# A fused attention and state-space kernel on one core: the causal masks of two head groups of segment 2 move to TensorE, and the written order changes in many small places

## The chip, the cores and the metric

The kernel runs on one core of one Trainium2 chip. The core has TensorE (matmuls, here PE, its weight loads PEld), VectorE (DVE), ScalarE (ACT), GpSimd (POOL) and SyncE (SP), which here only issues DMAs. Each engine works through its own list of instructions in order and waits on semaphores for the others. The metric is device microseconds of one execution of the whole program; lower is better.

## The reference, cut to what matters

Two branches read the same input x (2048 tokens, 512 channels), and a gate per token mixes them.

```python
def reference(...):
    g = sigmoid((x * gate_w).sum(-1, keepdims=True))
    a = _A_ref(x, wq, wk, wv, wo, beta)      # attention with a memory, 32 heads of 16
    b = _B_ref(x, ...)                       # state-space kernel K, long convolution, + u * Dskip
    return g * a + (1 - g) * b

# in _A_ref, for each of 4 segments s of 512 tokens:
    logits = einsum('bhqd,bhkd->bhqk', qs, ks) * scale + mask   # mask: -1e9 where query < key
    p = softmax(logits); a_dot = einsum('bhqk,bhkd->bhqd', p, vs)
    a_mem = (phi(qs) @ M) / (phi(qs) @ z + 1e-6)
    o = sigmoid(beta) * a_mem + (1 - sigmoid(beta)) * a_dot
    M, z = M + phi(ks)^T vs, z + sum(phi(ks))
# in _B_ref:
    K = (C * exp(dt*A*l) * dB summed over 128 states).real      # 512 channels x 2048 taps
    y = irfft(rfft(pad(u)) * rfft(pad(K)))[:2048]
```

## The kernel before, in words

**Two streams in one program.** The attention works by segment s (0 to 3) and group of eight heads hg (0 to 3). For each: projections of k and q (project, L1051), tokens' v (seg_tokens, L985), state update (seg_state, L1009), scores, exp, value matmuls and normalisation (scores, L1080), memory part and transposition of the output (ophase, L1270). The state-space branch computes powers of the poles (ssm_powers, L840), tables for the kernel K from them (tables, L1316, four chunks c, with "lag" matmuls), and a long convolution in three levels: a first level over all of x, stored to a scratch in HBM (x_level1, L908), then 32 blocks u (conv, L1406 on), each with a forward transform X, a kernel transform K (E for the first halves), a product Y on VectorE, an inverse V, and a store of V into one of two collecting tiles. The function finals forms sixteen output blocks: fin (first part of the attention output and skip), fir (collected inverses of blocks 0 to 15), fih (last group of heads), fis (those of blocks 16 to 31, so that it needs the last V), out (scaling). For the first eight of the sixteen blocks a half result is spilled to a tile by VectorE (xD, spl) so that the bank comes free; the other eight hold their bank.

**Scores.** A block of scores is written by TensorE into banks 0 to 3 (always these four), exp on ScalarE moves it to a tile pT in SBUF, and the value matmuls read pT. The other four banks serve all else. In segments 0 and 1 (4s + hg < ND) a variant called halves skips the masked half of the diagonal squares. In segments 2 and 3 five blocks per group of heads are worked, in an order that the list fixes: A0 and A1 (one diagonal square of 128 columns per row group), B0, C and B1 (two squares). The causal mask of a block is put on either before the exp by TensorE (the identity times the tile negm, which holds -30000 where the key is later) or after it by VectorE (pT times mask01):

```python
    pem = 4 * s + hg < NPM                                                       # L1089
            op("PE", c_pe("R", ...), f, r=[qT, kT, ko], w=[P], acq=[pT])         # L1228
            if pem:
                    for r in range(4):                                           # L1231
                        st = ent[1][2] if len(ent) > 1 else 0
                        i = mm(e, ap(P, r * 512, [[st, len(ent)], [1, 128]]), ap(ident, n=128),
                               ap(negm, dims=[[0, len(ent)], [1, 128]]), False, True)
            o = op("ACT", ("Ax", 2048), lambda e, ...: e.activation(pT, P, ACT.Exp, scale=0.25), r=[P], w=[pT])   # L1237
            if not pem:
              op("DVE", ("V2", 128 * nb), lambda e, ...: e.tensor_tensor(pT, pT, mask01, ALU.mult), r=[mask01], w=[pT])  # L1248
```

Matmuls of all kinds go through one helper (mm, L706), evictions from PSUM through another (evac, L225 on: L229 is ScalarE's copy, L230 VectorE's, L232 and L233 the scaled ones), and DMAs through a third (L225). So those lines gather many uses.

**The order.** build_graph makes 1808 operations and numbers them as it makes them. What each engine does in which order is written out in the string ORDER (from L375): one entry per operation, in one line of time for all engines. An entry is the number, then a or v where the operation may run on ScalarE or VectorE, then the buffers that it takes. `30/2` is operation 30 with buffer 2, `31a` operation 31 on ScalarE. Sched.replay (L238) walks the list: every engine's list, SP's DMA queue among them, is the entries of that engine in this order. Sched.emit (L267) turns the dependences, and the reuse of buffers and banks, into semaphore waits. A DMA that has to wait in SP's list holds all DMAs behind it.

Numbers that the prediction speaks of: 76, 88, 108 are shifts of the first, second and fourth pole power between partitions (SBUF to SBUF DMAs, pwc0.0, 0.1, 0.3; 108's power has index 3); 626 and 841 are the transposing loads of x for segments 2 and 3; 23 is the load of wk; 6 a small constant (ones); 1246 the store of the first-level result xl1.1, 1253 the eviction of xl1.3; 654 to 657 are scores, exp, mask and values of block A0 of segment 2, group 0, and so on up to 729 for group 1's B1; 1689 to 1692 are Y30, V30, V30's eviction and store.

Of the kernel before, what the change touches and what calls it, by code (L numbers as in the profile page):

```python
# [369 lines left out]
NPM = 8  # L370
# [11 lines left out]
141/6 214a 120 21 139/1 223a 228/0/0/0 1252/2/0 201 229 627/5 628 208/0 1253a 1257/0 140 1040v/0 1039v 1250a 216/3  # L382
217a 224 268 1044 225 1037v 1251 1038v 230 842/1 843 130v/6 271/2/1/1 413/1 256/0/0 1042/0 257 1045 151/2 152/7 1254/3
131 1041 153 132 258 231 311/0/2/2 143 1043 89/3 272 233/0/1 234 165/2 227 188 235 1255a 226 154v/7 269/1/1 238/0/2
239 1049 166v/8 312a 144 202/0 1050 270a 155 90 8/0 1237/3/1 156 1046 273 236/0 240 1239/1 1240a 237 241 99/1 1238a
1256 167 242/0/3 168 203/0 243 244 274 1051 1263/2/0 1264a 1047/0 1052 1265/1 101/3 1266a 163/2 357/3/2 287/0/1 288
1053 245 209/0 1048 100 246 1241 416/2 1278/1 289 417a 247/1 1056/0 358a 232/1/0 275 1054 276/0 250/0/3 251 252 400/2
401 1268/3/1 248 164 1270/1 249/0 175a/9 314/2/0 315a 253/0 254 1269a 283/0/3 284 1061 255 259 1055 1271a 1267 4/0 285
1260/2/0 1261a 1272 1258/3 176 177 1057 1259a 278/0/2 279 280 1062 1262 260 261/2 1273/1/1 1275/2 1276a 313 354/3/3/1
355a 316/2/0/0 1274a 1277 1063 301/0/0 1058 262 302 317 1059/0 281/3 263 264 303 403/0 1286/1/0 1287a 282 286 290 402  # L390
291 359/0/1/1 1060 360 319 318 1065 1066/0 295/0/2 292/3 1294/2/1 1295a 296 297 28/0 1067 320/1 361 1296/2 362 363
1068 1069/0 338/0/1 339 1299/0 293 1064 191/0 109/0 1070 1297a 364 1298 192/0 340 1071/2/0 1075/1 1076 1077 204 111/4
110 121/3 294/1 1079/0 1080 1081a 123/0 1072 1078a 205 1073 1074a 1083/0 1086v/0 1088a 1284/3 1285a 1090v/0 122 298/0
356 1087v 299 300 1094 1092/0 1089v 1095 136a/4 330/0/2 331 332 1085 135/6 112v/2 1091 304 1288 133/1 1279/1/1 472/2/1
473a 113 114 1093 305 321/0/3 1099 306/4 1084 1096 322 323 134 145/2 1100 1097/0 1082 405/3/1/0 406a 341/2 342 307
344/0/0 345 1281/3 346 1101 1280a 476/0 308 309 1098 1282a 1283 1102 420/0 1106/0 421a 326/0/1 327 426/1/0/0 146/7 328
# [138 lines left out]
def build_graph(nc, es, A_x, A_wq, A_wk, A_wv, A_wo, A_beta, B_A_re, B_A_im, B_B_re, B_B_im,  # L535
# [544 lines left out]
    def scores(s, hg, k0):  # L1080
# [7 lines left out]
        nv = {0: 0, 1: 0}  # L1088
        pem = 4 * s + hg < NPM  # L1089

# [558 lines left out]
```

## Time and profile before

| what | value |
|---|---|
| time, median of 3 runs | 292.19 us (289.7, 292.19, 292.36) |
| span of the profiled execution, first to last instruction | 287.5 us |
| that execution's own time | not recorded beside the span; the three runs are 2.2 to 4.9 us above it |
| mean granted TensorE clock | 0.987 |
| ScalarE exps of 2048 columns (L1237, segments 2 and 3) | 40, 76.0 us, 1899 ns each |
| VectorE mask multiplies (L1249, segments 2 and 3) | 40, 22.6 us, 577 ns each |
| evictions by ScalarE (L229) and VectorE (L230), all shapes | 155 and 49 |

Reading it: a row of a group has line, engine, operation, output and input with shape, count, then busy time, the mean length of one in ns, and the idle time ahead of them with what ended it. Matmuls are pipelined, so one's length contains latency that the next one covers. The chain is the work that ended last, followed backwards. In a table of stages each engine has its busy time and, in brackets, its count of instructions.

### The profile page before, as it was taken

The page shows a single profiled execution, that of the slowest core. Times are in us where ns is not written, and L with a number is a line of the kernel's source. Part 1 is how long each engine was busy: PE and PEld are TensorE (multiplying, and loading weights), DVE is VectorE, ACT ScalarE, POOL GpSimd, SP SyncE. Part 2 cuts the span into 40 slices and gives each one's busy share as a digit, 9 for nine tenths or more (in the row PEclk, how much of TensorE's full clock was granted, in tenths as well). Part 3 has the DMA queues.
Part 4 walks back from the last instruction along what each step waited for, and adds up shares of the span by engine and source line. Part 5 has one row for each costly group of instructions (what it writes and reads, how often), then busy time and mean ns, then how long its engine had stood idle before and what let it go on. Part 6 is the DMA issues. An engine that isn't in the chain of part 4 may idle for free.

```text
span 287.5 us, 9336 instructions
## 1 busy us (share of the span) xinstructions
PE 253.1 (88%) x3896; PEld 158.7 (55%) x3947; DVE 265.0 (92%) x617; ACT 254.6 (89%) x320; POOL 5.0 (2%) x10
## 2 busy tenths in 40 slices
PE   5767888787898989979999989999999999999992
PEld 2424454564556546756766657665555454555661
DVE  3998999999999999979999999999999999997782
ACT  5998999999999999989989999999999999983212
POOL 5000000000000000000000000000000000000000
PEclk9999899999999999979999999999999999999999
DMA  6996762421125256914643388585776795894224
GB/s 164 270 223 143 184 203 84 130 87 42 41 47 134 63 141 205 226 32 97 188 132 102 90 252 244 166 232 161 234 215 168 207 229 160 243 186 102 72 109 182
DMA packets 60187, 44.49 MB, mean 155 GB/s; under 512 B 36209, under 2 KB 53490, under 8 KB 60146
## 3 DMA queue, kind: packets, MB, share of 16 engines
q1 hardware_dynamic: 60146, 43.90, 57.0%
q8 instruction: 31, 0.51, 0.8%
q14 instruction: 10, 0.08, 0.1%
HBM read 22.09 MB, written 7.86 MB: 104 GB/s over the span
## 4 chain that ended last, share of the span: by engine, by line
ACT 35%; PE 28%; DVE 26%; issue 5%; DMA 3%; SPq 0%; DVEq 0%; ACTq 0%
PE psum L706 28%; ACT sb L1237 10%; ACT sb L229 10%; ACT sb L1190 8%; DVE sb L1346 7%; DVE sb L1355 3%; ACT sb L850 3%; DVE sb L230 2%; DMA sb<-sb 2%; DVE sb L1349 2%; DVE sb L1487 2%; DVE sb L1358 2%; DVE sb L1249 1%; DVE sb L1154 1%; ACT sb L1021 1%
## 5 line engine op out<-in xcount | busy, mean ns | idle before, releaser
L706 PE MATMUL psum<-sb 128*128 128x17 bf16 (+17 forms) x3808 | 247.4, 229 | 23.5 <-ACT sb L1190 7.4
L706 PEld LDWEIGHTS psum<-sb 128*128 128x128 bf16 (+6 forms) x3859 | 153.5, 102 | 115.5 <-issue 20.7
L229 ACT ACTIVATE sb<-psum 128x512 bf16<-128x512 f32 (+4 forms) x155 | 87.7, 624 | 7.6 <-PE psum L706 6.4
L1237 ACT ACTIVATE sb<-psum 128x2048 bf16<-128x2048 f32 x40 | 76.0, 1899 | 2.1 <-PE psum L706 1.7
L1190 ACT ACTIVATE sb<-psum 128x2048 bf16<-128x2048 f32 (+1 forms) x40 | 70.1, 1751 | 2.8 <-PE psum L706 2.7
L1346 DVE TENSOR_TENSOR sb<-sb 128x4096 bf16<-128x4096 bf16 (+3 forms) x24 | 37.7, 1569 | 0.0
L230 DVE CAST sb<-psum 128x512 bf16<-128x512 f32 (+1 forms) x49 | 29.9, 626 | 1.1 <-PE psum L706 0.9
L1355 DVE TENSOR_TENSOR sb<-sb 128x512 bf16<-128x512 bf16 (+1 forms) x48 | 25.0, 537 | 0.1
L1249 DVE TENSOR_TENSOR sb<-sb 128x1024 bf16<-128x1024 bf16 (+1 forms) x40 | 22.6, 577 | 0.2
L1487 DVE TENSOR_TENSOR sb<-sb 128x1024 bf16<-128x1024 bf16 x32 | 21.6, 685 | 0.9 <-ACT sb L229 0.5
L1349 DVE TENSOR_TENSOR sb<-sb 128x2048 bf16<-128x2048 bf16 (+3 forms) x24 | 20.7, 861 | 0.0
L232 ACT ACTIVATE sb<-psum,sb 128x512 bf16<-128x512 f32 x6 | 4.0, 687 | 12.3 <-PE psum L706 12.3
L1154 DVE TENSOR_TENSOR sb<-psum,sb 128x256 bf16<-128x256 f32 x32 | 13.3, 417 | 0.3
L1358 DVE TENSOR_TENSOR sb<-sb 128x512 bf16<-128x512 bf16 (+1 forms) x24 | 12.9, 536 | 0.0
L850 ACT ACTIVATE sb<-sb 128x512 f32<-128x512 f32 x18 | 11.8, 660 | 0.0
L1151 DVE RECIPROCAL sb<-psum 128x16 f32<-128x16 f32 x32 | 7.9, 252 | 1.8 <-PE psum L706 1.7
L1291 DVE TENSOR_TENSOR sb<-psum,sb 128x512 bf16<-128x512 f32 x12 | 8.2, 687 | 0.2
L858 ACT ACTIVATE sb<-sb 128x512 bf16<-128x512 f32 x12 | 8.0, 683 | 0.0
L1072 ACT ACTIVATE sb<-sb 128x512 bf16<-128x512 bf16 x12 | 8.0, 663 | 0.0
L1021 ACT ACTIVATE sb<-psum 128x512 bf16<-128x512 bf16 x12 | 7.8, 646 | 0.0
L852 DVE SCALAR_TENSOR_TENSOR sb<-sb 128x256 f32<-128x256 f32 x18 | 7.5, 424 | 0.0
L851 DVE TENSOR_TENSOR sb<-sb 128x256 f32<-128x256 f32 x18 | 7.5, 423 | 0.0
(78 smaller groups left out, 122.3 us busy)
## 6 DMA issues: line engine op xcount, KB each, us to landing
sb<-sb SPq DMA_DIRECT2D x64, 128.0 KB, 3.2
sb<-c_DN SPq DMA_DIRECT2D x32, 224.0 KB, 3.0
scr_Z<-sb SPq DMA_DIRECT2D x16, 256.0 KB, 3.2
sb<-scr_Z SPq DMA_DIRECT2D x16, 256.0 KB, 3.6
sb<-in_A_x_dram SPq DMA_DIRECT2D x5, 512.0 KB, 4.6
sb<-c_DN SPq DMA_DIRECT2D x16, 160.0 KB, 3.3
out_dram<-sb SPq DMA_DIRECT2D x8, 256.0 KB, 2.1
scr_O<-sb SPq DMA_DIRECT2D x12, 128.0 KB, 2.7
```

Source lines behind the costliest of these rows:

```text
L229: fa = lambda e: e.activation(dst(), src(), ACT.Copy)
L230: fd = lambda e: e.tensor_copy(dst(), src())
L706: mm = lambda e, o_, l, r_, st, sp, **kw: e.matmul(o_, lhsT=l, rhs=r_, start=st, stop=sp, skip_group_check=True, **kw)
L850: op("ACT", ("As", 512), lambda e, sq=sq, Z=Z: e.activation(ap(sq, n=512), ap(Z, n=512), ACT.Square), r=[Z], w=[sq], key=PW[h] + PWS * k)
L1190: o = op("ACT", ("Ax", 4 * n), lambda e: e.activation(ap(pT, dims=[[512, 4], [1, n]]), ap(P, dims=[[512, 4], [1, n]]), ACT.Exp, scale=0.25 ...
L1237: o = op("ACT", ("Ax", 2048), lambda e, P=P, pT=pT: e.activation(ap(pT, n=2048), ap(P, n=2048), ACT.Exp, scale=0.25), r=[P], w=[pT])
L1249: op("DVE", ("V2", 128 * nb), lambda e, pT=pT, dims=dims: e.tensor_tensor(ap(pT, dims=dims + [[1, 128]]), ap(pT, dims=dims + [[1, 128]]), ...
L1346: op("DVE", ("V2n1" if n == 1 else "V2", 512 * n), lambda e: e.tensor_tensor(ap(tile, 2 * dst, [[2 * (sp - dst), 2], [2 * ne, 128], [1, 2 ...
L1349: op("DVE", ("V2n1" if n == 1 else "V2", 256 * n), lambda e: e.tensor_tensor(D_(), D_(), ap(tile, 2 * sp + ne * 128, [[-ne * 128, 2], [2 * ...
L1355: op("DVE", ("V2x" if sstep > 2 else "V2", 256 * n), lambda e, half=half: e.tensor_tensor(run(t2, n, 0, 1) if half else run(tile, ne, dst, ...
L1358: op("DVE", ("V2", 256 * n), lambda e: e.tensor_tensor(D_(), D_(), ap(t2, n * 128, [[-n * 128, 2], [2 * n, 64], [1, 2 * n]]), ALU.add), r= ...
L1487: op("DVE", ("V2", 1024), lambda e, Y=Y, XAB=XAB, K3=K3, Ke=Ke, xo=xo, u=u: e.tensor_tensor(ap(Y, dims=[[512, 2], [1, 512]]), ap(XAB, xo, ...
```

## The change: masks of two groups, and the order

NPM goes from 8 to 10. With ND = 8 the groups below 8 take the variant halves and never reach the test, so the constant acts on 4s + hg = 8 and 9 alone: segment 2, groups 0 and 1. In each of their ten blocks the VectorE multiply goes, and four matmuls with the identity come between scores and exp. The count of operations stays 1808; in these ten blocks the number that was the exp's is now the mask matmul's and the number that was the multiply's is now the exp's.

ORDER is new throughout: every operation is still there once, most within some 20 places of where it stood. 45 of the 255 operations that may run on either engine change sides, 27 from ScalarE to VectorE and 18 the other way. Buffers are assigned anew. No other line changes. The diff, cut to NPM and to some lines of ORDER (start, the beginning of segment 2's blocks, and the end):

```diff
-NPM = 8
+NPM = 10
...
 ORDER = """
-9/0 0/0 15/0 16/0 10/1 66/0 29/0 32/0/0 38/1/0 39 33v 41/0 48/1 30/2 31a 40/2 13/2 12/3 47/3 11/4 17/3 43/4 50/5 42/6
-49/7 54/0 44 3/0 51 45 46 56/8 18 19 52 53 215/0 67/4 69/5 55/9 59/0 57/10 58 34/0/1 61/11 70v/0 60/12 64/0 68v 62/13
-71/0 72/1 27/0 14/5 36/6/2 74a/0 73 75 24/0 218/1 63 23/0 266/2/0/0 35a 186/2 220/0 85/3 83/1 84 1236/1 26/0 222/7 37a
-189/2 7/0 76 1244/5/0 181/4 1249/4/1 77/3 95/0 22/0 199/0 78/5 96/6 97 103/1 626/0 182/3 86v/1 1/0 184/0 841/0 79 221a
-87 88 106a/2 1242/0 219a 1243a 1245a 104/7 105 115/1 185/0 206/6 107 117/0 91/1 2/0 116 207/0 1246 118a/3 210/1/1/1
-211a 187/0 212 129/4 1247/0 65 6/0 108 20 127/1 200 128 119 190 1248a 399/0 5/0 183 267a 1036v/0 98v/4 142v/5 213/1/0
...
-1792 1790a 1793 1794 1747 1795a 1796
+16/0 15/0 38/4/0 39 9/0 0/0 32/6/0 10/1 30/2 66/0 69/3 33a 31a 48/0 41/1 40/2 47/3 43/4 27/0 42/5 26/0 13/2 49/6 14/3
+54/0 50/7 44 45 51 46 17/1 56/8 55/9 52 53 57/10 12/4 67/2 11/5 34/5/1 24/0 7/0 61/11 1236/1 70v/0 58/0 3/0 60/12 59
+1/0 64/0 62/13 73/1 68v 23/0 71/0 63 18 74a/0 35a 77/1 36/2/2 1242/0/0 72 218/4/0 206/7 79/2 83/2 19 85/3 22/0 186/4
+29/0 215 181/5 84 78 97/6 86a/1 203/0 1247/6/1 220/3 37a 91/7 184/3 95/0 75 96 199/0 182/2 87 189/1 200 190/0 841/0
+1244/5 105/0 65 207/0 103/0 104 76 219a 222/2 1245a 1248a 266/4/0/0 98a/2 210/5/1/1 115/1 221a 106v/3 118v/4 107 88
+117/1 1243a 626/0 267a 119 116 842/6 201 213/4/0 187/0 1249/7 216/3 202/0 127/1 129/5 211a 223a 268 128 183 1036v/0
+212 843 142v/5 108 139/1 130a/6 228/0/0/0 627/2 141/6 1038v 140 214a 6/0 143 131 1246 229 185 1250a 1257/0 231 628
...
+1806a 1807 1731 1786/4 1787 1746 1736 1705/3 1737/2 1706/0 1707 1713 1714 1715 1738 1791/1 1788 1792 1739 1793 1789/1
+1794 1795v 1747 1790a 1796
```

The evictions that change sides, by where they stand in time in the order before (an eviction has the name of its work; V5 is the inverse of block 5, K5 its kernel, X5 its transform):

| stage of before | from ScalarE to VectorE | from VectorE to ScalarE |
|---|---|---|
| 0 to 148 us | eight | eight |
| 148 to 208 us | tok3.0, lag3, lag3, pk2.3, V0, V1, K3, X11, V5, V6, V7 | E15, X13, X7, K4, K7 |
| 208 us to the end | V26, V27, V28, V29, V31, out8, out10, out13 | K27, K31, oT3.3, out9, out14 |

On TensorE the order at the end is, ahead of V30's inverse: fin2, fin9, fir9 earlier, fin5, fir3, fir5 later than before; behind it five held first halves (11, 14, 15, 12, 13) instead of seven (8, 11, 14, 9, 15, 12, 13) and two spilled ones (5, 4) instead of one (4).

More of the change, by code (lines that the diff above doesn't have):

```diff
@@ L381 @@
-211a 187/0 212 129/4 1247/0 65 6/0 108 20 127/1 200 128 119 190 1248a 399/0 5/0 183 267a 1036v/0 98v/4 142v/5 213/1/0
[L382 to L395, printed above, removed]
@@ new lines @@
+1548v 1420/0/2 1422/1 810 687 747 310 1447/0 1520v 807 1374/3/7 814/0/3 1392 1370/2 811 1411/2 1517 1423a 1421a
+850/1/2 808/0 812 1412v 815 1521/3 1526/2/0 754/0/0 813 851v 795/0 1527a 738 816 1503 1560/0 1522/1/1 1549/2 1378
+753/2 1496 1510 755 688 1416 1379a 1425 1528/0 817 855 802 1523v 1529/7/2 1375/4/0 818/3 1595/2 739 803 1371/1 819
+1440/0 1424 1376a 797/0 1530v 820/0 796 1550/2/0 1433/1 1561/3/1 1372a 756 1562a 1567/1 763/0/1 764 834/0/4/1 1596/3/2
+1551v 748/1 757/2 835 836 775/0/0 1597a 837 847/1/2/0 1381 1563/1 765 1564/0/3 776 854/0 1380 1565v 777 1598/3 770/3
@@ new lines @@
+935 1651/2 789 980 1672/3 1652/0/0 981 1461 954/0/3 982 961 1460 1649a 952 1465/3 1673/2/1 1653v 955 1466v 953/1
+1654/1 1674a 1472/0/2 956 967/0/1 1643 1658/0 1659/3/3 1655/2/3 968 1473v 1622 1660v 957 958 1656a 973 993/0/3 1470/0
+969 1467 962 1468 963/4 994 1471v 964 966/2 965/1 1675/0 970 974 940/3 975 25/0 976/0 1002/0/0 977 978 1693/2 941a
+1022/0/1/0 1003 1676/3/0 1023 983/2 984a 1024 1025 1708/0 1668/2 997/0/1 998 995 1657 1694/0/0 1677v 1756/0 1004
+1679/3 1709/1 996/2 1695a 1010/0/2 1475 1650 1710 1711 1680/3/1 1669/0/3 1615 1474 1750/1 1011 1014/0/3 1678 1701/1
```

138 lines of the change are left out of this document (70 added, 68 removed).

## The prediction

> **What bounds the kernel now.** I read the page's first section and the chain by engine first, then busy times by stage, then the chain in order of time.
>
> ```profile
> span 287.5 us, 9336 instructions
> PE 253.1 (88%) x3896; PEld 158.7 (55%) x3947; DVE 265.0 (92%) x617; ACT 254.6 (89%) x320; POOL 5.0 (2%) x10
> ACT 35%; PE 28%; DVE 26%; issue 5%; DMA 3%; SPq 0%; DVEq 0%; ACTq 0%
> ```
>
> No engine is the bound alone: three take turns on the chain. The stages say where each has room (columns: length, then busy us of PE, PEld, DVE, ACT, POOL with instruction counts, then clock, DMA share, GB/s).
>
> ```profile
> 0.00:27.00 27.00, 17.98 (x154) 9.39 (x157) 20.98 (x64) 22.30 (x44) 3.69 (x8) 1.00 0.91 206
> 148.00:180.00 32.00, 30.01 (x507) 19.47 (x512) 31.29 (x86) 31.39 (x37) 0.66 (x1) 1.00 0.59 167
> 180.00:208.00 28.00, 27.45 (x340) 17.30 (x344) 26.94 (x68) 27.86 (x32) 0.00 (x0) 1.00 0.69 197
> 208.00:250.00 42.00, 40.71 (x540) 22.12 (x546) 40.98 (x94) 41.26 (x42) 0.00 (x0) 1.00 0.74 200
> 264.00:283.00 19.00, 18.17 (x109) 11.32 (x109) 14.66 (x22) 5.06 (x8) 0.00 (x0) 1.00 0.43 136
> ```
>
> From 148 to 250 us all three are over 95% busy. At the end (264 to 283) VectorE and ScalarE have room and TensorE has none. The chain in order of time (start, length, work) gives the turns:
>
> ```profile
> 182.50 1.77 ACT sb L1237
> 184.91 4.95 PE psum L706 x76
> 202.65 4.01 PE psum L706 x39
> 207.63 0.59 DVE sb L1291
> 229.12 0.61 DVE sb L230
> 250.03 5.47 PE psum L706 x47
> 275.77 6.53 PE psum L706 x35
> 282.32 0.69 ACT sb L232
> ```
>
> ScalarE's exps carry it up to 184, TensorE to 208, VectorE to 230, and from 250 TensorE alone to 282.3. So time is won before 250 only if two engines give way together, and after 250 only if TensorE has less to do behind the last thing that it must wait for.
>
> **The masks.** Ten multiplies leave VectorE; in 147 to 180 us they are the only L1249 rows:
>
> ```profile
> L1249 DVE TENSOR_TENSOR sb<-sb 128x1024 bf16<-128x1024 bf16 x6 | 4.0, 688 | 0.0
> L1249 DVE TENSOR_TENSOR sb<-sb 128x512 bf16<-128x512 bf16 x4 | 1.6, 406 | 0.0
> ```
>
> That is 5.6 us off VectorE. In their place TensorE gets ten groups of four matmuls with the identity as weights: for A0 and A1 128 columns each, for B0, C and B1 256. Per group of heads 2 x 4 x 128 + 3 x 4 x 256 = 4096 columns, 8192 in all. The price of a column comes from the lengths of matmuls that differ only in columns, since a single length holds a fixed latency that the next one covers:
>
> ```profile
> L706 PE MATMUL psum<-sb 128*128 128x512 bf16 x461 | 119.7, 386 | 8.6 <-ACT sb L229 3.4 <-DVE sb L230 1.6 <-issue 1.3
> L706 PE MATMUL psum<-sb 128*128 128x128 bf16 x192 | 18.7, 224 | 0.0
> ```
>
> (386 - 224) / 384 = 0.42 ns per column, so 3.4 us on TensorE: 0.21 us for a group of 128s, 0.43 us for one of 256s. It could cost nothing, if it runs while TensorE would wait for evictions; as TensorE is idle for only 2.0 + 0.55 us of 148 to 208, it could cost all 3.4. I take nothing on the path from its length as such, because ScalarE is what carries the chain there; the cover is those idle 2.5 us and the time in which TensorE's queue waits for an eviction while earlier matmuls still show as busy; if it is gone, the 3.4 us are the price of the slower rival below.
>
> But the group stands between scores and exp, and all scores share one set of four banks, so the next exp waits for exp end, scores, mask, in a row:
>
> ```profile
> 148.65 1.88 ACT L1237 ACTIVATE sb<-psum 128x2048 bf16<-128x2048 f32 x1 [0.58 <-PE psum L706]
> 150.42 1.08 ACT L229 ACTIVATE sb<-psum 128x512 bf16<-128x512 f32 x2
> 151.37 1.90 ACT L1237 ACTIVATE sb<-psum 128x2048 bf16<-128x2048 f32 x1
> ```
>
> Here the exp ended at 150.53 and the next began at 151.37, 0.84 us later, with two evictions between that filled it. With the mask the turn takes about 0.84 + 0.21 or 0.43, so two evictions (1.08) nearly fill it and a single one does not. In the new order these exps have one short ScalarE instruction ahead of them: A1 of group 0, A0, B0 and C of group 1. That exposes 0.21 + 0.21 + 0.43 + 0.43 = 1.3 us; bounds 0 and 3.4. The wait from exp to the value matmul gets shorter by one VectorE instruction and its queue; VectorE's queue there is full of other work, so I count nothing for it.
>
> **Evictions that change engine.** Of 255 instructions with a choice, ScalarE has 175 now and 166 after. Up to 148 us the swaps cancel. Of those that stand between 148 and 208 now, eleven leave ScalarE (tok3.0, two lag3, pk2.3, V0, V1, K3, X11, V5, V6, V7) and five join it (E15, X13, X7, K4, K7): net six. From 208 on it is net three (V28, V27, V26, V31, V29 and three outputs leave; K27, K31, oT3.3 and two outputs join).
>
> ```profile
> L229 ACT ACTIVATE sb<-psum 128x512 bf16<-128x512 f32 x135 | 78.0, 628 | 7.3 <-PE psum L706 6.0 <-DMA scr_Z<-sb 1.1
> L230 DVE CAST sb<-psum 128x512 bf16<-128x512 f32 x38 | 25.5, 686 | 1.1 <-PE psum L706 0.9
> ```
>
> Busy time per instruction is 78.0 / 135 = 0.58 us on ScalarE and 25.5 / 38 = 0.67 us on VectorE. From 148 to 208 ScalarE loses 6 x 0.58 = 3.5 us and regains 1.3 us of gaps: 2.2 us shorter. VectorE loses 5.6 and gains 6 x 0.67 = 4.0: 1.6 us shorter. As they alternate on the chain, the smaller counts: 1.6 us. Bounds: 3.5 us if no gap opens and VectorE follows; a loss if evictions that now queue behind table work on VectorE hold TensorE's banks, at most the 3.4 us of the rival.
>
> **The start.** In the old order SP issues the store of a first-level result (1246) ahead of ones (6) and the shift of the third power (108), and all wait behind it:
>
> ```profile
> 21.12 1.20 SPq L225 DMA_DIRECT2D scr_Z<-sb  x1
> 22.36 0.47 SPq L225 DMA_DIRECT2D sb<-c_ones  x1
> 22.87 0.95 SPq L225 DMA_DIRECT2D sb<-sb  x1
> 23.87 2.04 SPq L743 DMA_TRANSPOSE sb<-in_A_x_dram  x1
> ...
> 25.92 0.30 DVE L230 COPY sb<-sb 128x256 bf16<-128x256 bf16 x1 [1.43 <-DMA sb<-sb]
> 25.39 1.58 ACT L229 ACTIVATE sb<-psum 128x512 bf16<-128x512 f32 x3 [1.14 <-DMA scr_Z<-sb]
> ```
>
> VectorE waits 1.43 us for 108, ScalarE 1.14 us for the buffer that 1246 empties. The new order issues 108 first and moves the waiting eviction (1253) behind the first exp. Against it: 108 now stands behind a transposing load of x (626), and such a load holds the queue for 2.04 us (the fourth row), wk is issued four places later, and the first exp needs the same TensorE work as before. I take 0.8 us; bounds 1.4 gained and 1.5 lost (a second wait of the old length). What the other small moves before 148 do I price at 0 with the same bounds.
>
> **The end.** The last wait is for block 30's inverse (V30): product on VectorE, two matmuls, eviction, DMA; only then can the second halves (fis) run.
>
> ```profile
> 261.38 0.26 DVE L1151 RECIPROCAL sb<-psum 128x16 f32<-128x16 f32 x1 [1.33 <-PE psum L706]
> 263.81 0.69 DVE L1487 TENSOR_TENSOR sb<-sb 128x1024 bf16<-128x1024 bf16 x1 [0.52 <-ACT sb L229]
> 266.04 0.60 ACT L229 ACTIVATE sb<-psum 128x512 bf16<-128x512 f32 x1 [1.61 <-PE psum L706]
> ```
>
> Summed record by record along the order, VectorE has 1.5 us more ahead of that product after than before (V31, V29, V26, xD2 and xD3 come first now); the idle 1.33 + 0.52 in these rows takes it up, so the product comes at about the same time, less what was won earlier. Behind V30 TensorE has less: before seven held first halves (2048 columns, 0.86 us each), one spilled (1536, 0.65), one transpose of 1024 (0.43) and 41 single matmuls (0.216): 16.0 us. After five, two, none, 41: 14.5 us. The 1.5 us that left run ahead of V30, where TensorE waits anyway if the earlier stages have gained; if not, they push V30 back. I take half of it, 0.7 us, with bounds 0 and 1.5. SP's moves here (loads for the spilled groups earlier, the store of V25 earlier, the transposes of segment 0's outputs later) each land long before their readers, and the two last outputs now leave on two engines at once: nothing either way. VectorE's eleven outputs and six additions of some 0.7 us fit into the 14 us behind V30.
>
> **The sum.** 0.8 + 1.6 + 0.7 = 3.1 us by terms, less 0.7 that I choose as an allowance: "issue" is 5% of the chain, 14.4 us that no engine's work explains, and a reordered chain will meet some of it anew, here a twentieth. That leaves 2.4 us. Span 287.5 - 2.4 = 285.1. The three runs of before are 2.2 to 4.9 us above that span; their median 292.19 lies 4.7 above it, so the forecast is 285.1 + 4.7 = 289.8 us. About 1% is what a measurement can tell from no change, 2.9 us: the forecast lies just inside.
>
> **A rule weighed.** The Trainium skill, "Perfetto Trace Analysis", section Identifying the Most-Contended Engine, holds matmul busy time to be a bad measure of room on TensorE and wants the weight loads' busy share. By that, 148 to 208 is 61% full ((19.47 + 17.30) / 60) where the matmul rows give 96%; the 3.4 us would vanish without a trace, and the slower rival with them. The chain speaks half against the rule: from 184.91 to 207 TensorE's matmuls are what the others wait for. So I leave the rival its chance.
>
> **Rivals.** *TensorE becomes the bound (slower).* The ten mask groups lie on the path from 148 to 208: TensorE is already 57.5 of 60 us busy there and carries 184 to 207. Then 3.4 us are added, VectorE and ScalarE only wait longer, and the end gives nothing back as V30 comes late: 292.2 + 3.4 = 295.6. It decides as soon as less than 0.5 us of the 3.4 runs in idle time, since 2.9 is 1%. Against it: the rows of ScalarE in the same stage, 31.39 of 32.
>
> *Everything adds up (faster).* The start gains its 1.4, the middle the mean of 3.5 and 1.6, the end 1.5: 1.4 + 2.6 + 1.5 = 5.5, so 286.7. For it: none of the three excludes another. Against it: three engines at 95% hand every gain on only in part.
>
> *VectorE gives it all back (no change).* 5.6 us of masks leave it and 9 x 0.67 = 6.0 of evictions come: it ends with the same 265 us, and it is the fullest engine. Then 292.2.
>
> **How the numbers follow.** Forecast 0.50 (its own range 288.2 to 291.2, of which 0.20 is over 1% faster and 0.30 within), everything adds up 0.16, gives back 0.10, TensorE bound 0.24. Faster 0.20 + 0.16 = 0.36, same 0.30 + 0.10 = 0.40, slower 0.24. The range goes from 286.0, a little under the best case, to 296.3, a little over the slower one, leaving under 0.1 on each side.
>
> **What would show it.** Right: VectorE busy about 264 to 265 us, ScalarE about 250, TensorE 256 to 257; no L1249 rows between 147 and 180; no idle over 1 us on VectorE or ScalarE at 24 to 26 us; ScalarE idle ahead of exps in the two groups adding up to 1 to 1.5 us; the PE piece of the chain that begins near 250 beginning near 248. Wrong: PE pieces of the chain between 148 and 180 where ScalarE's stood, or new waits of TensorE for L230, or a gap in TensorE's rows ahead of the first fis.

## The result: 1.6% slower, where about 1% faster was forecast

The changed kernel takes 293.9 us (median of 4 runs, 292.48 to 295.63) against 291.16 us of the kernel before on the same chip (4 runs, 289.7 to 292.36). The ratio on record is 1.0156, 95% interval 1.0112 to 1.0199: slower. The plain quotient of the two medians is 1.0094, so the direction is sure and the size less so. Ratios here and below use each kernel's faster executions alone, as a few ran over 1.5% longer than the fastest, mostly at a lower granted clock, and the profiles of e1 and e4 are of such slow ones. The forecast of 289.8 us had the wrong sign; 293.9 lies inside the range. The profiled execution took 294.57 us, its span is 292.8 us, so 1.8 us lie around the span; the span grew by 5.3 us.

The first section of the page after, and the chain by engine:

```profile
span 292.8 us, 9470 instructions
PE 264.5 (90%) x3987; PEld 162.4 (55%) x3987; DVE 265.4 (91%) x616; ACT 252.4 (86%) x311; POOL 5.0 (2%) x10
PE 46%; ACT 30%; DMA 12%; SPq 5%; DVE 4%; issue 2%; ACTq 0%
```

VectorE is as busy as before (265.4 after 265.0): the multiplies left and evictions came. TensorE's share of the chain went from 28% to 46%, VectorE's from 26% to 4%, and DMA has 12% where it had 3%. The stage of the moved masks, with the same columns as in the prediction:

```profile
148.00:180.00 32.00, 31.22 (x490) 20.11 (x487) 26.73 (x73) 27.89 (x28) 0.66 (x1) 1.00 0.66 163
```

From 148 to 180 VectorE fell from 31.29 to 26.73 us and ScalarE from 31.39 to 27.89: both idle, neither got ahead. The exps show where they idle. Timeline of ScalarE, then of the weight loads, in the first masked blocks after:

```profile
148.29 1.88 ACT L1237 ACTIVATE sb<-psum 128x2048 bf16<-128x2048 f32 x1 [0.40 <-PE psum L706]
151.13 1.88 ACT L1237 ACTIVATE sb<-psum 128x2048 bf16<-128x2048 f32 x1
154.29 1.88 ACT L1237 ACTIVATE sb<-psum 128x2048 bf16<-128x2048 f32 x1 [0.69 <-PE psum L706]
182.90 1.87 ACT L1237 ACTIVATE sb<-psum 128x2048 bf16<-128x2048 f32 x1
```

```profile
150.37 0.10 PEld L706 LDWEIGHTS psum<-sb 16*128 16x128 bf16 x4 [0.42 <-ACT sb L1237]
150.70 0.34 PEld L706 LDWEIGHTS psum<-sb 128*128 128x128 bf16 x6 [0.23 <-issue]
153.31 0.12 PEld L706 LDWEIGHTS psum<-sb 32*128 32x128 bf16 x8 [0.42 <-ACT sb L1237]
153.64 0.90 PEld L706 LDWEIGHTS psum<-sb 128*128 128x128 bf16 x20 [0.21 <-issue]
```

The scores' weights (16 or 32 rows) are loaded at 150.37 and 153.31, the mask's (128 rows) 0.33 us later, of which 0.21 to 0.23 us is a pause in the weight loads (the view's "issue": no wait that the profile shows), and the exp begins at 151.13 and 154.29. From scores to exp that is 0.76 us for a block with one square and 0.98 with two. Nine of the ten masked blocks show one of these two times within 0.01 us (the tenth, 1.08, found ScalarE still busy); the block without this mask that stands among them, A1 of group 2, shows 0.45. Before, it was 0.46:

```profile
148.19 0.12 PEld L706 LDWEIGHTS psum<-sb 16*128 16x128 bf16 x8 [0.22 <-DVE sb L1063]
148.52 0.46 PEld L706 LDWEIGHTS psum<-sb 128*64 128x64 bf16 x10 [0.21 <-issue]
```

(The exp of this block is the row at 148.65 in the prediction.) The pause is there before, too, but behind the scores, and the exp doesn't wait for what stands behind it. The mask draws it into the turn. A part of the pause is work: the scores' own columns still stream. The last score matmul of a block begins 0.14 us (128 columns), 0.20 (256) or 0.31 (512) ahead of the next 128-row weight load, and at the 0.42 ns per column of the prediction's rows 0.09 to 0.10 us are left over in each case.

The Trainium skill, "TensorEngine Tiling (Array Packing)", section Tiling Modes, Key Properties, says that a change of tiling mode drains TensorE. The rows agree in that each pause stands where the weights go from 16 or 32 rows to 128, with 0.09 to 0.10 us beyond the last column; no run here tried a mask that stays in the scores' mode.

To measure the stretch alone I take the time from the first exp of segment 2 to the exp of block A0 of group 3, behind the last masked block. (It holds nine of the ten masked turns, since the first lies ahead of the first exp.) Before it is 148.65 to this row, 30.95 us:

```profile
179.60 1.91 ACT L1237 ACTIVATE sb<-psum 128x2048 bf16<-128x2048 f32 x1
```

After it is 182.90 - 148.29 = 34.61 us: **3.66 us are lost here**. The rest, about 2 us, is lost between 205 and 245 us, where the chain has loads of the convolution's constants (c_DN); chain in order of time, after:

```profile
155.84 7.03 PE psum L706 x147
...
175.77 4.39 DMA sb<-scr_Z
...
208.28 4.74 DMA sb<-c_DN
...
226.82 1.87 SPq L225
...
230.49 4.74 DMA sb<-c_DN
...
244.95 3.57 DMA sb<-c_DN
...
255.35 32.15 PE psum L706 x261
```

(The load from scr_Z lies in the stretch; of its 4.39 us TensorE's weight loads show a wait of 0.4.) Comparing each instruction's start in the two traces, record by record, the changed kernel is 0.9 us ahead at 140 us, 3.0 behind at 180 and at 200, 3.9 at 210, 4.9 at 230 and 5.2 at 240; at the end it is 5.3, the difference of the spans. So nothing was lost behind 250, and nothing to speak of gained.

The granted clock matters for such comparisons. In most traces it drops to 0.50 for one or more pieces of 3.41 us: in the profile of before at 27.4 and 126.4 us, after at 65.7 for 6.83 us, each of them ahead of the stretch. A piece costs TensorE up to 1.7 us. The lead of 0.9 us at 140 is the drop of before at 126.4: between the exps at 126.5 and 130.0 us the changed kernel gains 0.83 us on it, and so, to 0.01 us, do the eight runs that have its order there (e3 to e6, e8, e10, e11, e16). In the stretch the clock is 1.00 in both, and ahead of it both have 6.8 us at half of it, so the 3.66 us are not the clock's.

### The profile page after: what moved, and what is told of

Read it like the earlier page. It is cut to its first block, busy times and chain, and to the rows that moved or that the text cites. A ratio compares the mean times of both kernels' runs of the same rounds, so it can differ in the third digit from the quotient of the medians.

```text
span 292.8 us, 9470 instructions
## 1 busy us (share of the span) xinstructions
PE 264.5 (90%) x3987; PEld 162.4 (55%) x3987; DVE 265.4 (91%) x616; ACT 252.4 (86%) x311; POOL 5.0 (2%) x10
## 4 chain that ended last, share of the span: by engine, by line
PE 46%; ACT 30%; DMA 12%; SPq 5%; DVE 4%; issue 2%; ACTq 0%
PE psum L706 46%; ACT sb L1190 12%; ACT sb L229 10%; DMA sb<-c_DN 4%; SPq L225 4%; DMA scr_Z<-sb 3%; DMA sb<-scr_Z 3%; ACT sb L850 3%; ACT sb L858 2%; ACT sb L1237 1%; DVE sb L230 1%; DMA sb<-in_B_A_im_dram 1%; DVE sb L1487 1%; ACT sb L1021 1%; ACT L928 0%
## 5 line engine op out<-in xcount | busy, mean ns | idle before, releaser
L706 PE MATMUL psum<-sb 128*128 128x17 bf16 (+18 forms) x3899 | 258.5, 231 | 20.2 <-ACT sb L1190 7.6
L706 PEld LDWEIGHTS psum<-sb 128*128 128x128 bf16 (+7 forms) x3899 | 156.1, 102 | 118.5 <-issue 23.9
L229 ACT ACTIVATE sb<-psum 128x512 bf16<-128x512 f32 (+5 forms) x147 | 83.9, 613 | 15.8 <-PE psum L706 13.2
L1237 ACT ACTIVATE sb<-psum 128x2048 bf16<-128x2048 f32 x40 | 75.1, 1877 | 4.9 <-PE psum L706 4.5
L230 DVE CAST sb<-psum 128x512 bf16<-128x512 f32 (+3 forms) x58 | 35.8, 630 | 6.0 <-PE psum L706 5.6
L1249 DVE TENSOR_TENSOR sb<-sb 128x1024 bf16<-128x1024 bf16 (+1 forms) x30 | 16.8, 574 | 0.1
L232 ACT ACTIVATE sb<-psum,sb 128x512 bf16<-128x512 f32 x5 | 3.3, 686 | 11.2 <-PE psum L706 11.2
L1557 DVE SCALAR_TENSOR_TENSOR sb<-psum,sb 128x512 bf16<-128x512 f32 x8 | 5.6, 744 | 2.2 <-PE psum L706 2.1
```

The source lines that it names most:

```text
L229: fa = lambda e: e.activation(dst(), src(), ACT.Copy)
L230: fd = lambda e: e.tensor_copy(dst(), src())
L706: mm = lambda e, o_, l, r_, st, sp, **kw: e.matmul(o_, lhsT=l, rhs=r_, start=st, stop=sp, skip_group_check=True, **kw)
L1237: o = op("ACT", ("Ax", 2048), lambda e, P=P, pT=pT: e.activation(ap(pT, n=2048), ap(P, n=2048), ACT.Exp, scale=0.25), r=[P], w=[pT])
L1249: op("DVE", ("V2", 128 * nb), lambda e, pT=pT, dims=dims: e.tensor_tensor(ap(pT, dims=dims + [[1, 128]]), ap(pT, dims=dims + [[1, 128]]), ...
```

## The experiments

Three theories. **Turn**: the mask lengthens the row exp, scores, mask, exp, which all blocks go through one after another. **Room**: TensorE has no time left for 8192 more columns, wherever they stand. **Order**: the new list loses by itself. The table gives each run's ratio to the kernel before and the stretch as defined above (30.95 us before, 34.61 after; a dash where it was not read). The stretches of e1, e2 and e10 contain 3.41 us at half the clock, worth up to 1.7 us; that of e9 ran at a granted clock of 0.95; the others at 1.00.

| run | ratio, 95% interval | stretch, us |
|---|---|---|
| e1 masks on TensorE at the exp's place, old order | 1.0405, 1.0344 to 1.0466 | 40.53 |
| e2 new order, masks on VectorE | 1.0294, 1.0233 to 1.0355 | 37.90 |
| e3 mask in the scores' step, multiply kept, old order | 1.0124, 1.0059 to 1.019 | 33.92 |
| e4 the same columns elsewhere | 1.006, 1.002 to 1.01 | 33.72 |
| e5 mask in the scores' step, no multiply, old order | 1.014, 1.0067 to 1.0214 | 33.93 |
| e6 no mask at all, old order | 0.9992, 0.995 to 1.0034 | 30.97 |
| e7 changed kernel, three transfers later | 1.0212, 1.0139 to 1.0284 | 34.94 |
| e8 e3 with 2 columns per matmul | 1.0092, 1.0051 to 1.0133 | 31.72 |
| e9 no mask at all, new order | 1.0168, 1.0113 to 1.0223 | 34.21 |
| e10 before, 8192 columns fewer | 1.0013, 0.9969 to 1.0057 | 31.09 |
| e11 e5, 8192 columns fewer | 1.0118, 1.0056 to 1.0181 | 33.40 |
| e12 to e15 parts of the new order alone | 1.0389 to 1.1152 | - |
| e16 old list to 148 us, new behind, no mask | 1.0206, 1.0147 to 1.0265 | 33.61 |
| e17 new list to 148 us, old behind, no mask | 1.0323, 1.0279 to 1.0367 | - |

### e1 and e2: each half alone

e1 keeps the old order and takes the masks to TensorE; the exp moves to the multiply's number, and the mask matmul stands at the exp's old place.

```diff
-NPM = 8
+NPM = 10
 ORDER (for each of the ten blocks)
-654 ... 655 ... 656 ... 657
+654 ... 655 656 ... 657
```

> The order of before; in the ten blocks the mask goes to TensorE, right behind the scores, and the exp keeps its place on ScalarE; VectorE loses the ten multiplies. Theory Turn (the mask lengthens the serial turn exp, scores, mask, next exp, because all scores share one set of banks): the trace of the changed kernel shows steps of 0.19 us (four groups) and 0.34 us (six groups), 2.8 us together, and scores to scores 2.9 us where before had 2.4 to 2.7; so +2.5 to +4 us here too, ScalarE idle 3 us or more between 148 and 180. Theory Order (the masks are harmless, the new order is what costs): 0 or a gain of up to 2 us, since VectorE is relieved by 5.6 us.

e2 is the new order with the masks on VectorE, each multiply eight entries ahead of its values.

```diff
-NPM = 10
+NPM = 8
 ORDER (for each of the ten blocks: mask matmul out, multiply in)
```

> The new order, with the ten masks multiplied by VectorE as before, each placed some eight entries ahead of the first value matmul that needs it. Theory Order: slower than before by most of the 4.5 us (ratio 1.0156), with VectorE now the fullest engine. Theory Turn: the 2.5 to 4 us between 147 and 180 are gone; VectorE has 5.6 us more there, so 0 to +2.5 us against before. What is lost behind 205 (about 2 us in the trace of after, at waits for DMAs of the constants c_DN) stays in both.

Both lost far more than either theory had said, and neither is a clean half. In e1 other matmuls stand between scores and mask; timeline of one block:

```profile
154.31 0.12 PEld L705 LDWEIGHTS psum<-sb 32*128 32x128 bf16 x8 [0.42 <-ACT sb L1236]
154.64 0.45 PEld L705 LDWEIGHTS psum<-sb 128*128 128x128 bf16 x5 [0.21 <-issue]
155.31 1.20 PEld L705 LDWEIGHTS psum<-sb 128*64 128x64 bf16 x52 [0.21 <-issue]
156.82 1.88 ACT L1236 ACTIVATE sb<-psum 128x2048 bf16<-128x2048 f32 x1 [1.80 <-PE psum L705]
```

The scores' weights were loaded by 154.43, the exp began at 156.82, for TensorE first did block E15 (154.64) and a piece of the "lag" work. A mask that isn't issued right behind its scores costs whatever stands between. In e2 the old multiplies stand in a list that was written without them.

### e3 and e4: the columns inside the turn and outside it

e3 puts the mask matmuls into the scores' own step and keeps the multiply, with the order of before. e4 puts the same forty matmuls at the head of other steps of the stretch, where they multiply into banks that the step overwrites.

```diff
 # e3, in the scores' step
+                if 8 <= 4 * s + hg < 10:
+                    for r in range(4):
+                        i = mm(e, ap(P, r * 512, [[st, len(ent)], [1, 128]]), ap(ident, n=128),
+                               ap(negm, dims=[[0, len(ent)], [1, 128]]), False, True)
 # e4, in tok3.0 to 3.2, pq2.1, pk2.3, pq2.3, X6, X7, X10, X12 (nx: 1 or 2)
+                for _ in range(4):
+                    i = mm(e, ap(P, n=128 * nx), ap(ident, n=128), ap(ident, dims=[[0, nx], [1, 128]]), True, True)
```

> The order of before and all its instructions; the ten mask groups on TensorE are added behind the scores, and the ten multiplies on VectorE stay too, so nothing is relieved. Theory Turn: +2.5 to +4 us, about the same as with the masks alone, since VectorE was not what the exps waited for. Theory Room (TensorE has no spare time between 148 and 208): +2.8 to +3.4 us. Theory Order: under 1 us.

> The order of before; the same number of matmuls and columns (ten groups of four, 8192 columns, identity as weights) is added between the same times, but at the head of token projections, projections and first transforms (X), whose own first matmul overwrites the result; they stand outside the turn from exp to exp. Theory Room: +2.8 to +3.4 us as with both masks. Theory Turn: under 1.2 us, as TensorE does them while ScalarE is in an exp.

e3 loses 2.97 us in the stretch, with nothing taken off VectorE and nothing moved: the added matmuls alone do it. e4 loses 2.77 us there in its profiled execution, but that one took 295.43 us, 3.4 above the median of its thirteen; by the ratio e4 loses 0.6%, 1.7 us, about half of e3's 1.24%, and the two intervals overlap. This lies between what Turn (under 1.2) and Room (2.8 to 3.4) had said, so it settles neither; e10 and e11 tried Room from the other side.

### e5 and e6: the multiply is worth nothing

e5 is e3 without the multiplies; e6 is the kernel before without them, and without any mask in those ten blocks.

```diff
 # e5 and e6: no multiply for groups 8 and 9
-            if not pem:
+            if not pem and not 8 <= 4 * s + hg < 10:
```

> Order of before; the mask matmuls of the ten blocks stand in the scores' own step, as in e3, and VectorE's ten multiplies are gone (e3 kept them). Turn and Room both say the multiply was covered and TensorE's addition decides: as e3, 1.0 to 1.5% over before (292.5 to 294), exp-to-exp from the first to the tenth masked block about 28.7 us against 25.8 of before. If VectorE's relief counts, 1.5 to 3 us under e3 (within 0.5% of before). If the masks only hurt in e1 because they stood at the exp's place of the order, behind other matmuls (up to 1.5 us of them in that trace), this run must be some 7 us or more below e1 (under 294).

> Order of before; the ten blocks have no mask at all, neither matmul nor multiply (the kernel leaves out the causal mask of those blocks). What the 5.6 us taken off VectorE are worth alone. Prediction on record for evictions and relief in 148 to 208 was 1.6 us. If VectorE's list was on the path there: 2 to 4 us under before (286 to 288). If it was covered by the turn of exp and scores and by TensorE: within 0.7 us of before.

e6 takes the time of before, 0.9992 (0.995 to 1.0034), although VectorE has 4.3 us less in the stretch:

```profile
148.00:180.00 32.00, 30.15 (x497) 19.58 (x502) 26.97 (x76) 31.98 (x36) 0.66 (x1) 1.00 0.61 167
```

ScalarE is busy for 31.98 of 32 us: in the old order it bounds this stretch, and what VectorE no longer does falls into idle time. So in the old order no way of masking these ten blocks could have won more than the 0.5% that the interval leaves. e5 (33.93 us) is e3 (33.92) to the hundredth: dropping the multiplies gave nothing back. The rows of e5's first exp and of the one behind the blocks:

```profile
147.33 1.88 ACT L1241 ACTIVATE sb<-psum 128x2048 bf16<-128x2048 f32 x1 [1.17 <-PE psum L705]
181.26 1.93 ACT L1241 ACTIVATE sb<-psum 128x2048 bf16<-128x2048 f32 x1
```

### e8, e10 and e11: step or columns

```diff
 # e8: e3 with 2 columns per mask matmul
-                        i = mm(e, ap(P, r * 512, [[st, len(ent)], [1, 128]]), ap(ident, n=128),
-                               ap(negm, dims=[[0, len(ent)], [1, 128]]), False, True)
+                        i = mm(e, ap(P, r * 512, n=2), ap(ident, n=128), ap(negm, n=2), False, True)
 # e10 and e11: tok3.0 to tok3.3, and pq2.1 and pk2.3 (k0_ = 2)
-                for k in range(4):
+                for k in range(3 * (s == 3), 4):
...
-                for k in range(4):
+                for k in range(k0_, 4):
```

> As e3 (order of before, multiply kept), but each of the forty mask matmuls has 2 columns in place of 128 or 256, so that it adds to TensorE 80 columns in place of 8192 and keeps the extra step with its weight load inside the turn. Turn by the step itself (0.21 us from the scores to the mask's first weight load, in every masked block of the changed kernel): 1.5 to 2 us over before. Room (columns): within 0.5 us of before.

> The kernel before, with 8192 columns taken off TensorE outside the turns but in the stretch 148 to 180: one matmul of four is left in each token projection tok3.0 to tok3.3, two of four in pq2.1 and pk2.3 (the kernel leaves out parts of these projections; no step is removed). Room (TensorE's columns are priced in full there, e4 had plus 8192 columns at plus 0.6%): 1.5 to 3 us under before. Turn alone: as before.

> As e5 (masks on TensorE inside the scores' step, no multiplies, order of before), with the 8192 columns of e10 taken off elsewhere in the same stretch, so that TensorE's columns there are those of before (parts of those projections are left out). Room with the step inside the turn (e8: 0.9%, of which 0.9 us in the stretch): 0.3 to 1 us over before in the stretch, 2 to 3.5 us under e5. Turn alone: as e5, 1.4% over before.

e10 takes the time of before and e11 that of e5, both within their intervals: 8192 columns taken off TensorE outside the turn bring nothing that can be told, with the mask or without. In the stretch e11 has 0.53 us less than e5, both at the full clock. e10 has 0.14 more than before, but its clock was at half from 148.0 to 151.4 us, and over all executions its mean granted clock is a little lower (0.982 against 0.986), so a gain of 1 to 2 us by e10 is not excluded. Stages of e11:

```profile
148.00:180.00 32.00, 27.77 (x484) 19.27 (x486) 24.58 (x70) 29.52 (x31) 0.65 (x1) 1.00 0.51 143
```

All three engines idle here (27.77, 24.58 and 29.52 of 32 us), and the stretch still takes 33.40 us, 2.45 more than before. TensorE and ScalarE wait for each other; waits of e11 in 147 to 182 us (us in all, times, longest):

```profile
PEld psum L705 <- ACT sb L1243: 6.1, 7, 1.6
...
ACT sb L1243 <- PE psum L705: 2.9, 6, 1.2
```

With the columns in (e5) these are 3.1 and 3.4: the time taken off TensorE's work came back as TensorE's wait for the exps. No engine's work bounds the stretch; the serial turn does. **Room falls** as the main cause: of e5's 2.98 us in the stretch, the columns taken off elsewhere give back 0.53. Why e4's columns cost anything wasn't tried by itself; my reading is that they went in front of work that the scores stand behind in TensorE's list, and so held up the turn.

e8 prices the parts of the turn. The scores' weights and the exp of a block with two squares:

```profile
149.77 0.12 PEld L706 LDWEIGHTS psum<-sb 32*128 32x128 bf16 x8 [0.42 <-ACT sb L1240]
150.10 0.55 PEld L706 LDWEIGHTS psum<-sb 128*128 128x128 bf16 x9 [0.21 <-issue]
150.40 1.88 ACT L1240 ACTIVATE sb<-psum 128x2048 bf16<-128x2048 f32 x1
```

From scores to exp 0.63 us, 0.17 more than without a mask, nearly without columns; full masks add 0.13 to 0.35 us to that. In the stretch e8 loses 0.77 us, e3 2.97: in these two profiles about a quarter comes with the step and its pause, three quarters with the columns inside the turn. Over the whole kernel e8 is 0.9% slower, some 2 us more than in the stretch, and its interval overlaps that of e3; this profile (span 286.7 us, no drop of the clock ahead of its last 3 us) doesn't show where the rest of that lies.

### e7: SP's queue behind 205 us

```diff
 ORDER
-1462/1 ... 1700/0 ... 1637/2 ... 1748/1 ... 1467      (Zx14, xr0, CD23, xr6, X29)
+1637/2 1462/1 ... 1467 1700/0 1748/1
```

> The changed kernel; only three transfers of SP's queue are put behind the c_DN load CD23 and later: the store Zx14 behind CD23, the loads xr0 and xr6 behind the loads X29 at 247. In the changed kernel's trace they stand in front of CD23 (Zx14 held the queue 1.87 us), and the loss against before grows from 3.0 us at 200 to 5 to 6 us at 240 and after. If SP's order makes that: 1 to 2 us under the changed kernel (292 to 293). If the loss after 205 only follows from the loss before it: same as the changed kernel.

(xr6 stood just behind CD23, not in front of it.) No gain: 1.0212 against the changed kernel's 1.0156, with intervals that overlap. Record by record its loss at 230 to 245 us does sink, from 4.9 to 5.2 us to 4.3, but at 250 the moved loads hold the queue in their new place; chain in order of time, e7:

```profile
247.57 0.58 SPq L225
...
248.19 0.45 SPq L225
...
248.68 4.57 DMA sb<-sb
```

and it is 5.7 us behind again. The wait moved with the transfers. So moving these three transfers does not undo the loss; whether SP's order makes it stays open.

### e9 and e12 to e17: the new order by itself

e9 is the changed kernel without any mask in the ten blocks: the mask matmuls are taken out of the list, nothing else.

```diff
-NPM = 10
+NPM = 8
-            if not pem:
+            if not pem and not 8 <= 4 * s + hg < 10:
 ORDER (ten mask matmuls out)
```

> The changed kernel's order, and the ten blocks have no mask at all (the kernel leaves out the causal mask of those blocks). If the whole loss is the mask on TensorE (e5 with the order of before: 1.014): 0.99 to 1.005 of before, and the changed kernel's 1.0156 is that mask. If the new order loses by itself (2 us behind 205 in the changed kernel's trace): 1.005 to 1.012. If the new order with VectorE's relief gains the 1.6 us of the prediction: 0.99 to 0.995.

It is 1.0168: as slow as the changed kernel. So **the new order loses by itself about what the mask loses by itself in the old order, and the two don't add**: 1.014 (mask alone), 1.0168 (order alone), 1.0156 (both), each within 0.4 to 0.7%. Its waits in 147 to 182 us, TensorE's on VectorE and the exps' on TensorE (us in all, times, longest; this execution ran at a granted clock of 0.95 throughout, five others at 0.979 to 0.988 took as long):

```profile
PEld psum L705 <- DVE sb L230: 2.0, 6, 0.4
...
ACT sb L1236 <- PE psum L705: 1.6, 2, 1.1
...
PEld psum L705 <- DVE sb L1044: 1.2, 1, 1.2
...
PEld psum L705 <- DVE sb L1357: 0.9, 1, 0.9
```

and the same view of the kernel before and of the changed kernel:

```profile
PEld psum L706 <- DVE sb L230: 0.3, 1, 0.3
```

```profile
ACT sb L1237 <- PE psum L706: 3.6, 8, 0.7
...
PEld psum L706 <- DVE sb L230: 0.5, 2, 0.4
```

In the new order without masks TensorE waits for VectorE: for evictions (L230), of which VectorE's list took some over, and once each for a step of the state (L1044) and of the tables (L1357). With the mask in, TensorE's wait for evictions is 0.5 us, and instead the exps wait 3.6 us for TensorE (1.6 without): one loss takes the place of the other. That the later exps are what gives VectorE its time is my reading; no run tried it by itself.

Then I tried which part of the new order it is. All of these have no mask in the ten blocks.

```diff
 # e12: order of e6, the engine letters a/v of the 45 evictions as in the changed kernel
 # e13: order of e9, those letters as before
 # e14: order of e6, SP's entries in the changed kernel's sequence
 # e15: order of e6 to the scores of 2.0.C (one block of scores 22 entries later, other buffers in 158 entries), then that of e9
 # e16: as e15, with before's first 945 entries exactly (9 buffers renumbered behind them)
 # e17: first 935 entries of e9, then the order of e6 (9 buffers renumbered)
```

> Order of before, no mask in the ten blocks (as e6, which took the time of before), and every eviction with a choice on the engine that it has in the changed kernel (45 of 255 change). The prediction's step on record: ScalarE and VectorE both shorter, 1.6 us gained (0.994 of before). If these changes are what loses in e9: 1.008 to 1.017. If the loss lies in positions (SP's, TensorE's): 0.997 to 1.003.

> The mirror: order of the changed kernel, no mask (as e9, 1.0168), and every eviction on the engine that it has before. If the evictions lose: back to 1.000 to 1.006. If positions lose: 1.012 to 1.02.

> Order of before on the four engines, no mask (as e6), and SP's queue of transfers in the order of the changed kernel (a few buffers of the pools are numbered otherwise). The prediction had SP's moves at nothing. If they are what loses (the c_DN and scr_Z loads that TensorE waits for at 175, 208, 230 and 245 in the changed kernel's trace): 1.008 to 1.017. If not: 0.997 to 1.004.

> No mask; the order of before, with its evictions, as far as the first block of segment 2, and from there the order and evictions of the changed kernel (some buffers are numbered otherwise). If what loses in e9 lies behind 148: 1.012 to 1.018. If it lies in the moves ahead of 148, whose loss the traces show only later: 0.997 to 1.005.

> No mask in the ten blocks. The list of before entry by entry, buffers included, as far as the first block of segment 2 (945 of 1798 entries, about 148 us), and from there the changed kernel's order and engines (9 buffers numbered otherwise; in e15 55 were, and its time was lost ahead of 148, where the order was that of before). If the loss of e9 is made behind 148: 1.010 to 1.018, and lags as before's up to 148. If it comes from the moves ahead of 148: 0.997 to 1.004.

> The mirror, no mask: the changed kernel's list as far as the first block of segment 2 (935 entries), then the order and engines of before (9 buffers numbered otherwise). The prediction had 0.8 us gained at the start and the small moves up to 148 at nothing: 0.994 to 1.000. If the loss of e9 comes from the moves ahead of 148: 1.010 to 1.018.

e12 is 1.0671, e13 1.0389, e14 1.1152, e15 1.0715: all far outside both expectations. A choice taken over from one list into the other is worse here than either list. Why is open, and the clock has a part in it: the mean granted clock of their executions is 0.93 to 0.98 where before has 0.98, and in e15's profile it is at half for 30.7 us ahead of 148 us (before: 6.8). That can be worth up to 15.4 us, and e15's first exp of segment 2 comes 16.4 us later than that of before (165.06 against 148.65), although its order up to there is that of before but for one block of scores. So e15 tells nothing of its question, and whether such a list loses by its waits or by the clock that comes with them wasn't separated. These four settle nothing, except that here a part of the order couldn't be priced by transplanting it.

e16 can be read, because it only joins two lists at a cut: 1.0206. In the stretch it takes 33.61 us, 2.66 more than before, and TensorE waits for VectorE's evictions there (147 to 185 us):

```profile
PEld psum L705 <- DVE sb L230: 3.8, 7, 1.5
```

Against e6, record by record, it loses 2.5 us more from 140 to 180, another 1.0 by 200 and 1.1 by 230. e17 loses 9 us once at its seam, 7.3 of them in a wait of TensorE for a load of c_DN, and from there runs beside the old order to the end (7.3 us behind at 160, 6.6 at 280): behind 148 the old list loses nothing. Up to the seam e17 is not behind e6 either. So the new order's own loss is made behind 148 us. Which moves behind 148 make it stays open beyond the waits for VectorE.

## Why the prediction was wrong, point by point

**The masks: this step failed first.** The prediction wrote "I take nothing on the path from its length as such, because ScalarE is what carries the chain there", and let 1.3 us of the turn be exposed, at four of ten blocks; even these then fell out of the sum, which took VectorE's 1.6 us as the smaller gain. The columns were priced rightly (two squares cost 0.98 - 0.76 = 0.22 us more than one, for 512 columns). But the turn grew by 0.30 us (0.76 - 0.46) and 0.52 (0.98 - 0.46), 0.09 more than the 0.21 and 0.43 priced, which is the part of the pause beyond the scores' columns. Above all the cover was wrong: of the 4 x 0.30 + 5 x 0.52 = 3.8 us in the nine masked turns of the stretch some 3.0 were exposed (e5 33.93 - 30.95), not 1.3. The cover, ScalarE's evictions between exp and exp, was counted by its length. But ScalarE was full (31.98 of 32 us in e6), with gaps between exps only as long as its evictions, so a turn that outgrows them leaves ScalarE idle: 3.6 us ahead of exps after, 0.6 before. That ScalarE carries the chain is a reason to price a longer turn in full, not at nothing.

**The multiplies.** VectorE's relief was what let the next step gain at all; e6 shows that in the old order it is worth nothing that can be told (0.9992). The reasoning "as they alternate on the chain, the smaller counts" needed VectorE to be in the way in this stretch, and ScalarE at 31.98 of 32 us in e6 shows that it was not.

**The evictions.** Forecast 1.6 us gained; measured the other way. The prediction had named the mechanism as a bound ("evictions that now queue behind table work on VectorE hold TensorE's banks") and did not choose it. e16's 3.8 us of TensorE's waits for L230 are a sign of it, and its 2.66 us of loss lie within the 3.4 us given. How much of that loss the swaps make, and how much other moves, no run separates, since e12 and e13 could not be read; in the changed kernel, with the mask in, these waits are only 0.5 us.

**SP's moves.** The prediction had looked at SP's queue only near the start and the end (its "nothing either way" is said of the end), and had no term for 205 to 245, where c_DN loads stand in the chain three times and about 2 us are lost. e7 does not show that SP's order makes this loss, so its cause stays open.

**The start.** The two waits that it named are gone, and a new one of nearly their length stands in their place, within the bound given for a second wait; timeline after:

```profile
24.68 1.01 PE L706 MATMUL psum<-sb 128*128 128x1 bf16 x24 [1.04 <-DMA sb<-in_A_x_dram]
```

TensorE now waits 1.04 us for x. At 30 to 50 us the changed kernel is 0.8 to 1.2 us ahead, at 100 level. The profile of before ran at half the clock from 27.4 to 30.8 us, which alone can be worth up to 1.7 us, and runs whose lists are the same up to 147 us (e3, e5, e6, e8, e16) differ by some 4 us at 100, so 0.8 us can't be told.

**The end.** 0.7 us forecast; the lag goes from 5.3 us at 250 to 5.3 at the end: nothing. But the wait for block 30 is gone: from 255.35 TensorE runs 32.15 us without a break.

**The offset.** The sum added 4.7 us to the span, which is the profile's span set against the median of three executions. The 209 executions on record whose span is known lie 1.7 to 2.2 us above their own span, so the 4.7 mixes this with the spread between executions; that 289.8 lies near the medians of before is no support for the terms.

**The rivals.** "TensorE becomes the bound" had the sign and nearly the time (295.6), at 0.24. Its mechanism was in the main not what happened: e10 and e11 show that TensorE's time as such was hardly short, so the nearness of its time is luck. The rule weighed from the Trainium skill ("Perfetto Trace Analysis", Identifying the Most-Contended Engine) was right that TensorE at 96% by its matmul rows still had room (e11). What the prediction drew from it, that the masks would vanish, was wrong: what they cost is latency in a turn, which neither share shows. Of the signs listed, VectorE's 265.4 us came about as said, and ScalarE's 252.4 lies a little over the 250. TensorE's 264.5 is far from the 256 to 257 said. ScalarE waited 3.6 us ahead of exps, where 1 to 1.5 was said, and a PE piece of the chain at 155.84, between 148 and 180, was the sign for wrong.

## What to carry to other kernels

When an operation goes from behind a link of a serial turn to inside it, price it by the time from the turn's one end to the other, pauses included, and count the whole of it as soon as the engine that carries the turn is full. First measure what the thing taken away is worth by leaving it out (e6): zero there ends the argument before any order is changed. In a list fitted by hand or by a search, changes need not add up or come apart (e9, e12 to e15): test a new list whole, or joined to the old one at one cut with its buffers kept. And look at the granted clock of both traces before comparing their times.

## What the runs showed of the hardware that I had not expected

A group of matmuls on 16 or 32 rows, followed by one on 128 rows, leaves a pause of 0.21 to 0.23 us in the weight loads, in every such pair in 147 to 180 us of the traces before and after, even within one step and with 2 columns (e8). The next load begins 0.09 to 0.10 us after the scores' last column, counted at 0.42 ns each; the rest of the pause is the scores' own columns. Ten thin steps lengthen the turns by 10 x 0.17 = 1.7 us, where the columns of the full masks add 4 x 0.13 + 6 x 0.35 = 2.6 us.

Executions with identical lists up to 147 us lie up to 4.5 us apart at 100 us (e8 2.1 us ahead of the profile of before, e16 2.5 behind). The granted clock goes with it: up to 100 us e8 has no drop, before one of 3.41 us to 0.50, e16 one of 10.24 us, worth up to 0, 1.7 and 5.1 us of TensorE's time. What makes the clock drop wasn't looked into.
